# Parameter rows on GpSimd's queue, two more of the first weight strips on ScalarE's queue, and the first six GELUs ahead of the table sines

## The chip, the cores and the metric

The kernel runs on one core of one Trainium2 chip. The time is the device time of one execution in microseconds (us); lower is better. Before the change it is 216.26 us in the median of the 4 executions that were timed beside the changed kernel (216.15 to 216.58). The profiles show one execution each; the profiled span of the kernel before is 214.7 us, a little less than its time, because the span runs from the first to the last instruction.

Names used below: PE is TensorE, DVE is VectorE, ACT is ScalarE, POOL is GpSimd, SP is SyncE, which issues most of the DMAs. In the profile, PEld is PE's weight loads, and a q behind a name (SPq) is that engine's sequencer, which waits and issues. A "bank" is one of the eight PSUM banks of this kernel, into which PE writes. The "granted clock" is the share of full speed at which PE was allowed to run. In the code P is 128, a chunk has TPC = 4 tiles of 128 rows (H = 2, HT = 256), 640 columns are KD = KS = 5 blocks of 128, the 1728 are KF = 14 (the last one partial), and FA = 6 of these come first.

## The reference

The input x has 2048 rows of 640. The output mixes two branches with a gate computed from x:

```python
g = sigmoid((x * gate_w).sum(-1, keepdims=True))
# branch A: a diagonal complex state space model, 640 states
dt = exp(log_dt);  Lam_bar = exp(dt * Lam);  B_bar = ((Lam_bar - 1) / Lam)[:, None] * Bmat
h_t = Lam_bar * h_{t-1} + B_bar @ x_t            # a scan over the 2048 rows
a   = 2 * real(C @ h) + x * Dskip
# branch B: a dense layer, 640 -> 1728 -> 640
b   = gelu(x @ w1 + b1) @ w2 + b2
out = g * a + (1 - g) * b                        # bf16
```

## The kernel before

The rows are handled in four chunks of 512. The complex scan is made real by rotating with tables of cosines and sines (`TCOS`, `TSIN`), which the kernel itself builds at the start: ScalarE computes four small sine activations, and DVE multiplies them out. PE, DVE and ScalarE run in an order that is fixed by hand; SP's order is left to the framework.

The start: x's first chunk comes in four strips and is transposed on PE; `w1a` (the first 768 columns of w1) comes in five strips, `w1b` (the rest) in five more.

```python
load_xn(0, 0, 1)
load_w1a(nc.scalar, 0)
load_xn(0, 1, 2)
load_w1a(nc.scalar, 2)
...                                               # a tiny Exp, to load its table
load_xn(0, 2, 3)
load_xn(0, 3, 4)
rows(nc.sync, prmA[0:KS, :], A_log_dt)            # parameter rows, 1.2 to 3.2 KB each
rows(nc.sync, prmA[KS:2 * KS, :], A_Lambda_im)
rows(nc.sync, prmA[2 * KS:3 * KS, :], A_Lambda_re)
for kd in (1, 4, 3):
    load_w1a(nc.sync, kd)
rows(nc.sync, prmB[KS:NB, :], B_b1[0:(KF - 1) * P])
rows(nc.sync, prmB[0:KS, :], gate_w)
for kd in range(KD):                              # w1b
    nc.sync.dma_start(out=w1b[kd][:, 0:F - cut1], in_=B_w1[kd * P:(kd + 1) * P, cut1:F])
```

PE's order at the start is a mix of `strip` (matmuls of one w1a strip into six open banks) and `turn_all` (transposes of one x strip). The parameter rows are transposed by one matmul each (`prmA` gives `colA`, `prmB` gives `colB`, the GELU biases). Then come the four sines, then the six first GELUs:

```python
nc.scalar.activation(out=FS[...], in_=red,     func=ACT.Sin, ...)
nc.scalar.activation(out=FC[...], in_=ab,      func=ACT.Sin, ...)
nc.scalar.activation(out=sq[:],   in_=redq[:], func=ACT.Sin, ...)
nc.scalar.activation(out=cq[:],   in_=absq[:], func=ACT.Sin, ...)
for kf in range(FA):
    ...                                           # at kf == 3: prmB is transposed, colB copied
    for kd in (4, 3):
        ff1_mm(banks[kf], 0, kf, kd, 0, CH, False, 3)
for kf in range(FA):
    ff1_act(banks[kf], 0, kf)                     # GELU with bias colB: bank -> gel
...
nc.vector.tensor_tensor(out=m1, in0=FC[:, :, lo], in1=over(cQ), op=ALU.mult)   # DVE's first product with cq
```

`fold` rescales C in five steps; ScalarE makes two products in a pair of buffers (`ft`, `bufs=2`), DVE uses them:

```python
def fold(ks):
    t1 = fwork.tile([P, D], F32, name="ft", bufs=2)
    t2 = fwork.tile([P, D], F32, name="ft", bufs=2)
    nc.scalar.activation(out=t1[:], in_=CT_im[:, ks, :], func=ACT.Identity, scale=n2im[:, ks:ks + 1])
    nc.scalar.activation(out=t2[:], in_=CT_re[:, ks, :], func=ACT.Identity, scale=n2im[:, ks:ks + 1])
    ...                                           # DVE: CT_re <- CT_re * c2re + t1, CT_im <- CT_im * n2re + t2
```

`seed(ti)` lets DVE write x times Dskip into a bank, into which PE then accumulates the final tile `ti`; `fin_a` makes the output tile `ot` on DVE and stores it. `ot` has two buffers, and the loads of the next x chunk are issued right after:

```python
def fin_a(c, at={}):
    for a in range(TPC):
        ot = fwork.tile([P, D], BF16, name="ot", bufs=2)
        if a < TPC - 2:
            seed(ti + 2)
        ...                                       # matmuls; DVE: ot <- bank * gate + gb
        nc.sync.dma_start(out=out2d[ti * P:(ti + 1) * P, :], in_=ot[:])
...
fin_a(0)
load_xn(2, 0, H)
load_xn(2, H, TPC)
ssm(2, {KS - 1: lambda: first_banks(1)})
```

Of the kernel before, what the change touches and what calls it, by code (L numbers as in the profile page):

```python
# [11 lines left out]
ACT = mybir.ActivationFunctionType  # L12
# [4 lines left out]
P = 128  # L17
T = 2048
D = 640
F = 1728  # L20
CH = 512
NCH = T // CH
KD = D // P
KS = D // P
KF = (F + P - 1) // P
F_LAST = F - (KF - 1) * P
NT = T // P
TPC = CH // P
H = TPC // 2
HT = H * P  # L30
KSA = 2
HD = D // 2
FA = 6

MAGIC = 12582912.0
TWO_PI_M = float(np.float32(2.0 * np.pi * (1.0 - 2.0 ** -20)))
# [5 lines left out]
def kernel(  # L42
# [19 lines left out]
    nc = tc.nc  # L62
# [12 lines left out]
    def bank(dtype=F32):  # L75
        return ps.tile([P, CH * 4 // (4 if dtype == F32 else 2)], dtype, name="bank")


    cut1 = FA * P
    n1b = F - cut1 + 1  # L80
    xT = [const.tile([P, KD, CH], BF16, name=f"xT{c}") for c in range(NCH)]
    w1a = [const.tile([P, cut1], BF16, name=f"w1a_{kd}") for kd in range(KD)]
    w1b = [const.tile([P, n1b], BF16, name=f"w1b_{kd}") for kd in range(KD)]
# [6 lines left out]
    ident = const.tile([P, P], BF16, name="ident")  # L90
    prmA = const.tile([P, P], BF16, name="prmA")
    NB = KS + KF - 1
    prmB = const.tile([P, P], BF16, name="prmB")
    colA = const.tile([P, 3 * KS], F32, name="colA")
    colB = const.tile([P, NB], F32, name="colB")
# [10 lines left out]
    halfpi = const.tile([P, 1], F32, name="halfpi")  # L106
# [8 lines left out]
    def load_xn(c, a0=0, a1=TPC, queue=None):  # L115
        if a0 == 0:
            xn[c] = xnp.tile([P, TPC, D], BF16, name="xn")
        r0 = c * CH + a0 * P
        (queue or nc.sync).dma_start(out=xn[c][:, a0:a1, :], in_=x2d[r0:r0 + (a1 - a0) * P, :].rearrange("(a p) d -> p a d", p=P))

    def load_w1a(queue, kd):
        queue.dma_start(out=w1a[kd][:], in_=B_w1[kd * P:(kd + 1) * P, 0:cut1])

    def rows(queue, dst, v):
        queue.dma_start(out=dst, in_=v.rearrange("(j p) -> j p", p=P))  # L125
# [2 lines left out]
    load_w1a(nc.scalar, 0)  # L128
    load_xn(0, 1, 2)
    load_w1a(nc.scalar, 2)  # L130
    warm = const.tile([P, 1], F32, name="warm")
    nc.scalar.activation(out=warm[:], in_=nc.const_aps.tensor(1.0, [P, 1], BF16), func=ACT.Exp)
    load_xn(0, 2, 3)
    nc.vector.memset(prmA[:], 0.0)
    nc.vector.memset(prmB[:], 0.0)
    load_xn(0, 3, 4)
    rows(nc.sync, prmA[0:KS, :], A_log_dt)
    rows(nc.sync, prmA[KS:2 * KS, :], A_Lambda_im)
    rows(nc.sync, prmA[2 * KS:3 * KS, :], A_Lambda_re)
    for kd in (1, 4, 3):  # L140
        load_w1a(nc.sync, kd)
    rows(nc.sync, prmB[KS:NB, :], B_b1[0:(KF - 1) * P])
    rows(nc.sync, prmB[0:KS, :], gate_w)
    for kd in range(KD):
        nc.sync.dma_start(out=w1b[kd][:, 0:F - cut1], in_=B_w1[kd * P:(kd + 1) * P, cut1:F])  # L145
    make_identity(nc, ident[:])
    HC = CH // 4
    tfi = work.tile([P, HC], I32, name="e")
    nc.gpsimd.iota(tfi[:], pattern=[[1, HC]], base=0, channel_multiplier=0)
    nc.gpsimd.memset(b1x[:, F_LAST:F_LAST + 1], 0.0)  # L150
    span4 = const.tile([P, 4], F32, name="span4")
    for i, m in enumerate((1.0, float(CH), float(2 * HC), float(HC))):
# [5 lines left out]
    nc.sync.dma_start_transpose(out=xT[1][:], in_=x2d[CH:2 * CH, :])  # L158
    nc.sync.dma_start_transpose(out=CT_re[:], in_=A_C_re[:, :])
    nc.sync.dma_start_transpose(out=CT_im[:], in_=A_C_im[:, :])  # L160
    for k0, k1 in ((0, 3), (3, 6), (6, 9), (9, KF - 1)):
        nc.sync.dma_start(out=w2_sb[:, k0:k1, :], in_=B_w2[k0 * P:k1 * P, :].rearrange("(kf p) d -> p kf d", p=P))
    for h in range(2):
        nc.sync.dma_start(out=w2l[h * F_LAST:(h + 1) * F_LAST, :], in_=B_w2[(KF - 1) * P:F, :])
# [1 line left out]
    nc.sync.dma_start(out=Dbc[:], in_=A_Dskip.rearrange("(o d) -> o d", o=1).to_broadcast([P, D]))  # L166
    nc.sync.dma_start_transpose(out=xT[2][:], in_=x2d[2 * CH:3 * CH, :])
    nc.sync.dma_start_transpose(out=xT[3][:], in_=x2d[3 * CH:4 * CH, :])
    for a in (0, H):
        load_xn(1, a, a + H)  # L170

    ctx.enter_context(tc.manual_schedule(engines={E.PE, E.DVE, E.Activation}))

# [39 lines left out]
    pA = bank()  # L213
# [43 lines left out]
    def ff1_act(p, c, kf):  # L257
        nc.scalar.activation(out=gel[c][:, kf, :], in_=p[:, :], func=ACT.Gelu_apprx_tanh, bias=b1_c[:, kf:kf + 1])  # L258
        act(0.69)
# [51 lines left out]
    def strip(kd, t0, t1, first, f0=0, f1=FA):  # L311
        for kf in range(f0, f1):
            ff1_mm(banks[kf], 0, kf, kd, t0, t1, first, 3)

    def turn_all(a):
        tB = bank()
        for i in range(3):
            turn(tB, i * P, a, i)
        turned(nc.vector, tB, 0, a, 0, 1)
        turned(nc.vector, tB, P, a, 1, 3)  # L320
        for i in range(2):
            turn(pA, i * P, a, 3 + i)
        turned(nc.scalar, pA, 0, a, 3, 5)
# [2 lines left out]
    turn_all(1)  # L326
    strip(2, 0, P, False)
    strip(0, P, HT, True)
    nc.tensor.matmul(pA[:, HT:HT + 3 * KS], lhsT=prmA[:], rhs=ident[:, 0:3 * KS], start=True, stop=True, skip_group_check=True)
    nc.vector.tensor_copy(out=colA[:], in_=pA[:, HT:HT + 3 * KS])  # L330
    nc.scalar.activation(out=dt16[:], in_=ldt_c, func=ACT.Exp)
    strip(2, P, HT, False, 0, 3)
    turn_all(2)
    nc.vector.tensor_copy(out=dt32[:], in_=dt16[:])
    nc.vector.tensor_tensor(out=dtl[:], in0=dt32[:], in1=lre_c, op=ALU.mult)
    nc.vector.tensor_tensor(out=th_c[:], in0=dt32[:], in1=lim_c, op=ALU.mult)
    nc.vector.tensor_scalar(out=thp_c[:], in0=th_c[:], scalar1=INV_2PI, scalar2=None, op0=ALU.mult)
    strip(2, P, HT, False, 3, FA)
    strip(0, HT, HT + P, True)
    turn_all(3)  # L340
    nc.scalar.activation(out=r_c[:], in_=dtl[:], func=ACT.Exp)
    strip(2, HT, HT + P, False)
    strip(0, HT + P, CH, True)
    strip(2, HT + P, CH, False)
    strip(1, 0, CH, False)


    HB = 2 * HC
# [4 lines left out]
    u, red, ab = scratch(0), scratch(1), scratch(2)  # L353
    m1, m2 = scratch(3), scratch(4)
    FSC = hsp.tile([P, 2 * KS, HB], F32, name="hs")
    FS = FSC[:, 0:KS, :]
    FC = FSC[:, KS:2 * KS, :]
# [3 lines left out]
    redq = col("redq", n=NQ * KS)  # L361
    absq = col("absq", n=NQ * KS)
    sq = col("sq", n=NQ * KS)
    cq = col("cq", n=NQ * KS)
# [11 lines left out]
    sQ, cQ = sq[:, 3 * KS:4 * KS], cq[:, 3 * KS:4 * KS]  # L376


    nc.scalar.activation(out=FS[:, :, 0:HC], in_=red, func=ACT.Sin, scale=TWO_PI_M)
    nc.vector.scalar_tensor_tensor(out=ab, in0=red, scalar=-1.0, in1=red, op0=ALU.mult, op1=ALU.max)  # L380
    nc.scalar.activation(out=FC[:, :, 0:HC], in_=ab, func=ACT.Sin, scale=-TWO_PI_M, bias=halfpi[:])
    nc.vector.tensor_tensor(out=two[:].rearrange("p (n k) -> p n k", n=NQ), in0=thp_c[:].rearrange("p (o k) -> p o k", o=1).to_broadcast([P, NQ, KS]),
                            in1=span4[:].rearrange("p (n o) -> p n o", o=1).to_broadcast([P, NQ, KS]), op=ALU.mult)
    nc.vector.tensor_copy(out=kq[:], in_=two[:])
    nc.vector.tensor_tensor(out=redq[:], in0=two[:], in1=kq[:], op=ALU.subtract)
    nc.vector.scalar_tensor_tensor(out=absq[:], in0=redq[:], scalar=-1.0, in1=redq[:], op0=ALU.mult, op1=ALU.max)
    nc.scalar.activation(out=sq[:], in_=redq[:], func=ACT.Sin, scale=TWO_PI_M)
    nc.scalar.activation(out=cq[:], in_=absq[:], func=ACT.Sin, scale=-TWO_PI_M, bias=halfpi[:])
    for kf in range(FA):
        if kf == 3:  # L390
            nc.tensor.matmul(pA[:, 0:NB], lhsT=prmB[:], rhs=ident[:, 0:NB], start=True, stop=True, skip_group_check=True)
            nc.vector.tensor_copy(out=colB[:], in_=pA[:, 0:NB])
            for j in range(KD):
                nc.vector.tensor_copy(out=w1b[j][:, n1b - 1:n1b], in_=pA[:, j:j + 1])
        for kd in (4, 3):
            ff1_mm(banks[kf], 0, kf, kd, 0, CH, False, 3)
    for kf in range(FA):
        ff1_act(banks[kf], 0, kf)
    two_banks = [bank(), bank()]
    for kd in range(KD):  # L400
        for i in range(2):
# [278 lines left out]
    ff1(2, 0, {1: lambda: fold(3), 4: lambda: fold(4), 9: lambda: seed(0), 11: lambda: seed(1)})  # L680
    gates(2)
    fin_a(0)
    load_xn(2, 0, H)
    load_xn(2, H, TPC)
    ssm(2, {KS - 1: lambda: first_banks(1)})
    fin_b(1, seeds(1))
    fin_a(1)
    load_xn(3, 0, H)
    load_xn(3, H, TPC)
    ssm(3)  # L690
    gel_tile(3)
    ff1(3, 0, {KF - 3: lambda: first_banks(2)})
# [36 lines left out]
```

## Time and profile before

| | before |
|---|---|
| time, median of 4 | 216.26 us |
| span of the profiled execution | 214.7 us |
| PE busy | 209.7 us, 98% |
| DVE busy | 190.2 us, 89% |
| sines done (end of the one at 12.53 us), first GELU | 12.83 us, 14.14 us |
| DVE's first product with `cq` | 12.86 us |

The profile page of before gives the busy time of each engine, and the shares of the chain of waits that ended last:

```profile
span 214.7 us, 3536 instructions
...
PE 209.7 (98%) x1366; PEld 117.1 (55%) x1385; DVE 190.2 (89%) x396; ACT 101.4 (47%) x183; POOL 1.1 (0%) x12
...
PE 93%; DMA 3%; SPq 1%; issue 1%; DVE 0%
```

PE is the limit, but DVE is close behind it. DVE's order is fixed, so a delay at its start travels on until a moment at which it would have waited anyway.

The timeline of ScalarE in before; columns are start, duration (both us), engine, line, operation and tiles, and in brackets the idle time before it and what ended it:

```profile
8.66 1.28 ACT L379 ACT_TABLE_LOAD   x1
10.83 0.74 ACT L379 ACTIVATE hs<-gel 128x640 f32<-128x640 f32 x1 [0.88 <-DVE gel L372]
...
12.53 0.30 ACT L388 ACTIVATE cq<-absq,halfpi 128x20 f32<-128x20 f32 x1
12.84 1.28 ACT L258 ACT_TABLE_LOAD   x1
14.14 0.69 ACT L258 ACTIVATE gel<-bank,colB 128x512 bf16<-128x512 f32 x1
```

The sine table is loaded at 8.66 us, while the first sine still waits for DVE until 10.83.

The timeline of PE in before, the one place at the start where PE waits for a weight:

```profile
12.97 1.89 PE L253 MATMUL bank<-xT,w1b 128*128 128x512 bf16 x8
15.09 1.25 PE L253 MATMUL bank<-xT,w1b 128*128 128x512 bf16 x5 [0.23 <-DMA w1b<-in_B_w_dram]
```

The timeline of DVE in before: the product that needs `cq`, and the three longest waits of its steady part.

```profile
12.86 0.83 DVE L408 TENSOR_TENSOR gel<-hs,cq 128x640 f32<-128x640 f32 x1
...
76.19 0.89 DVE L459 SCALAR_TENSOR_TENSOR CT_re<-CT_re,c2re,ft 128x640 bf16<-128x640 bf16 x1 [0.38 <-ACT ft L455]
...
88.12 0.17 DVE L551 TENSOR_SCALAR gcol<-gz 128x4 f32<-128x4 f32 x1 [0.88 <-ACT gz L285]
...
97.34 0.55 DVE L658 SCALAR_TENSOR_TENSOR ot<-bank,gcol,gb 128x320 bf16<-128x320 f32 x1 [0.33 <-DMA out_dram<-ot]
```

The last one is a wait for a buffer of `ot`, whose store has not landed. The table of waits of before between 60 and 110 us (total, times, longest) has one more line for the argument: ScalarE waits 1.2 us for DVE to free an `ft` buffer, without any effect on PE.

```profile
ACT ft L453 <- DVE CT_re L459: 1.2, 1, 1.2
```

### The profile page before, as it was taken

To read this page: it belongs to the slowest core of one execution; us is meant where nothing else is said; L and a number is where in the kernel's file an instruction comes from. 1 tells how busy PE (TensorE), PEld (TensorE's weight loads), DVE (VectorE), ACT (ScalarE), POOL (GpSimd) and SP (SyncE) were. 2 spreads that over 40 slices of the span, in tenths; PEclk is the share of its full clock that TensorE was granted. 3 is DMA by queue.
4 is the path that set the end of the run, shared out by engine and by line. 5 is a ranking of instruction groups with operands and counts; after the bars stand their busy time and mean duration, and the time that the engine had idled before them with its cause. 6 is when DMAs were issued, how large, how long until landed. Compare 5 with 4: busy or idle time off the path is not lost.

```text
span 214.7 us, 3536 instructions
## 1 busy us (share of the span) xinstructions
PE 209.7 (98%) x1366; PEld 117.1 (55%) x1385; DVE 190.2 (89%) x396; ACT 101.4 (47%) x183; POOL 1.1 (0%) x12
## 2 busy tenths in 40 slices
PE   8999999999999999999999999999999999999994
PEld 4745444454455644775445577444454567654774
DVE  2899999999999999899999999999999999983153
ACT  3599556665875696302572310356683423204200
POOL 1000000000000000000000000000000000000000
PEclk9999999999999999999999999999999999999999
DMA  6899999993000000051000005100000000100011
GB/s 201 251 177 232 219 220 374 170 225 92 3 0 0 3 2 0 12 183 64 0 0 3 0 0 186 61 2 0 0 3 14 0 3 31 61 31 3 0 66 61
DMA packets 30419, 15.84 MB, mean 74 GB/s; under 512 B 22978, under 2 KB 30402, under 8 KB 30402
## 3 DMA queue, kind: packets, MB, share of 16 engines
q1 hardware_dynamic: 29970, 15.18, 29.3%
q10 hardware_dynamic: 432, 0.43, 0.6%
q8 instruction: 11, 0.18, 0.3%
q14 instruction: 6, 0.05, 0.1%
HBM read 7.48 MB, written 2.62 MB: 47 GB/s over the span
## 4 chain that ended last, share of the span: by engine, by line
PE 93%; DMA 3%; SPq 1%; issue 1%; DVE 0%
PE bank L594 26%; PE bank L253 23%; PE bank L653 20%; PE bank L536 20%; DMA w1b<-in_B_w_dram 3%; PE bank L215 1%; PE bank L610 1%; PE bank L279 1%; SPq L145 1%; PE bank L218 0%; SPq L125 0%; DVE ot L658 0%; DVE xT L225 0%; PE bank L269 0%
## 5 line engine op out<-in xcount | busy, mean ns | idle before, releaser
L594 PE MATMUL bank<-w_sb,gel 128*128 128x128 bf16 (+1 forms) x408 | 56.9, 297 | 0.7 <-issue 0.5
L594 PEld LDWEIGHTS <-gel 128*128 128x128 bf16 x416 | 32.2, 98 | 25.5
L539 ACT ACTIVATE bu<-bank 128x512 bf16<-128x512 f32 x40 | 23.9, 597 | 39.4 <-PE bank L536 39.3
L258 ACT ACTIVATE gel<-bank,colB 128x512 bf16<-128x512 f32 x52 | 34.1, 694 | 11.9 <-PE bank L253 11.1
L653 PEld LDWEIGHTS <-hs 128*128 128x128 bf16 x330 | 31.6, 98 | 11.5
L490 DVE TENSOR_TENSOR_SCAN g<-r_c,carry,v 128x512 bf16<-128x512 f32 x30 | 37.4, 1272 | 0.0
L602 ACT ACTIVATE gb<-bank,gcol 128x512 f32<-128x512 f32 (+1 forms) x32 | 15.1, 527 | 35.4 <-PE bank L610 19.3
L253 PE MATMUL bank<-xT,w1b 128*128 128x512 bf16 x137 | 31.0, 379 | 0.4 <-DMA w1b<-in_B_w_dram 0.2
L253 PE MATMUL bank<-xT,w1a 128*128 128x512 bf16 (+1 forms) x152 | 27.7, 334 | 0.2
L653 PE MATMUL bank<-CT_re,hs 128*128 128x320 bf16 (+2 forms) x165 | 27.1, 295 | 0.0
L653 PE MATMUL bank<-CT_im,hs 128*128 128x320 bf16 (+2 forms) x165 | 27.1, 295 | 0.0
L658 DVE SCALAR_TENSOR_TENSOR ot<-bank,gcol,gb 128x320 bf16<-128x320 f32 (+2 forms) x33 | 17.6, 535 | 9.2 <-PE bank L653 8.7
L536 PE MATMUL bank<-xT,BT_im 128*128 128x512 bf16 x99 | 24.8, 379 | 0.1
L536 PE MATMUL bank<-xT,BT_re 128*128 128x512 bf16 x97 | 24.4, 379 | 0.2
L253 PEld LDWEIGHTS <-w1b 128*128 128x128 bf16 x140 | 13.6, 98 | 16.9 <-DMA w1b<-in_B_w_dram 0.7
L253 PEld LDWEIGHTS <-w1a 128*128 128x128 bf16 x156 | 13.8, 101 | 12.5
L569 DVE TENSOR_TENSOR bank<-xn,Dbc 128x320 f32<-128x320 bf16 (+2 forms) x33 | 14.5, 483 | 3.5 <-ACT gb L602 3.4
L536 PEld LDWEIGHTS <-BT_im 128*128 128x128 bf16 x100 | 9.8, 98 | 11.8
L471 DVE TENSOR_TENSOR v<-wa,wb 128x512 bf16<-128x512 bf16 x40 | 15.2, 421 | 0.6
L536 PEld LDWEIGHTS <-BT_re 128*128 128x128 bf16 x100 | 9.6, 98 | 11.0
L583 ACT ACTIVATE bank<-b2bc 128x512 f32<-128x512 bf16 (+1 forms) x24 | 11.7, 529 | 6.2 <-DVE ot L658 6.2
L471 DVE TENSOR_TENSOR wa<-TCOS,g 128x1024 bf16<-128x1024 bf16 x20 | 13.7, 687 | 0.1
(100 smaller groups left out, 151.5 us busy)
## 6 DMA issues: line engine op xcount, KB each, us to landing
out_dram<-ot SPq DMA_DIRECT2D x15, 160.0 KB, 1.8
xn<-in_A_x_dram SPq DMA_DIRECT2D x6, 320.0 KB, 3.2
w_sb<-in_B_w_dram SPq DMA_DIRECT2D x3, 480.0 KB, 4.0
w1b<-in_B_w_dram SPq DMA_DIRECT2D x5, 240.0 KB, 6.1
xn<-in_A_x_dram SPq DMA_DIRECT2D x4, 160.0 KB, 3.1
w_sb<-in_B_w_dram SPq DMA_DIRECT2D x1, 640.0 KB
w1a<-in_B_w_dram SPq DMA_DIRECT2D x3, 192.0 KB, 2.9
w1a<-in_B_w_dram ACTq DMA_DIRECT2D x2, 192.0 KB, 3.6
```

What stands on the lines that cost most here:

```text
L253: nc.tensor.matmul(p[:, t0:t1], lhsT=w, rhs=xT[c][:, kd, t0:t1], start=(kd == 0) if first is None else first, stop=(kd == last), skip_grou ...
L258: nc.scalar.activation(out=gel[c][:, kf, :], in_=p[:, :], func=ACT.Gelu_apprx_tanh, bias=b1_c[:, kf:kf + 1])
L471: nc.vector.tensor_tensor(out=o, in0=a, in1=b, op=op)
L490: nc.vector.tensor_tensor_scan(s["g"][:, ri, :], r_c[:, ks:ks + 1].to_broadcast([P, CH]), s["v"][:, ri, :], init, ALU.mult, ALU.add)
L536: nc.tensor.matmul(p[:], lhsT=BT[ks >= KSA][:, kd, (ks % KSA if ks < KSA else ks - KSA) * P:][:, 0:P], rhs=xT[c][:, kd, :], start=(kd == 0 ...
L539: nc.scalar.activation(out=bu[:, ri, :], in_=p[:], func=ACT.Identity)
L569: dve_now(ck.pe, 0.45, lambda: nc.vector.tensor_tensor(out=p[:, 0:d1 - d0], in0=xn[c][:, a, d0:d1], in1=Dbc[:, d0:d1], op=ALU.mult))
L583: nc.scalar.activation(out=v, in_=src, func=ACT.Identity)
L594: nc.tensor.matmul(p[:, col:col + d1 - d0], lhsT=gel[c][:, kf, a * P:(a + 1) * P], rhs=w2_sb[:, kf, d0:d1], start=False, stop=False, skip_ ...
L602: nc.scalar.activation(out=gbs[ti][:, d0:d1], in_=p[:, col:col + d1 - d0], func=ACT.Identity, scale=gcol[:, 1, ti:ti + 1])
L653: nc.tensor.matmul(p[:, 0:d1 - d0], lhsT=hs[c][:, j, lo:lo + P], rhs=CT[:, j % KS, d0:d1], start=False, stop=(j == 2 * KS - 1), skip_group ...
L658: nc.vector.scalar_tensor_tensor(out=ot[:, d0:d1], in0=p[:, 0:d1 - d0], scalar=gcol[:, 0, ti:ti + 1], in1=gbs[ti][:, d0:d1], op0=ALU.mult, ...
```

## The change

The intent: take small DMAs off SP's queue so that the weights are issued earlier; close the first six banks and let ScalarE empty them before the sines, so that PE gets banks back sooner; and spread loads over more pieces.

```diff
 load_w1a(nc.scalar, 2)
+load_w1a(nc.scalar, 1)
+load_w1a(nc.scalar, 4)
 ...
-rows(nc.sync, prmA[0:KS, :], A_log_dt)                 # and the two others
-for kd in (1, 4, 3):
-    load_w1a(nc.sync, kd)
-rows(nc.sync, prmB[KS:NB, :], B_b1[0:(KF - 1) * P])    # and gate_w
+load_w1a(nc.sync, 3)
 ...                                                    # w1b on nc.sync, as before
+rows(nc.gpsimd, prmA[0:KS, :], A_log_dt)               # and the four others, on nc.gpsimd
 ...
-for k0, k1 in ((0, 3), (3, 6), (6, 9), (9, KF - 1)):                       # w2
+for k0, k1 in ((0, 2), (2, 4), (4, 6), (6, 8), (8, 10), (10, KF - 1)):
 ...
-for a in (0, H):
-    load_xn(1, a, a + H)
+load_xn_in_3(1)                                        # three pieces; also for chunks 2 and 3
 ...
 strip(0, P, HT, True)
+strip(2, P, HT, False, 0, 3)
+turn_all(2)
+strip(2, P, HT, False, 3, FA)
 nc.tensor.matmul(pA[...], lhsT=prmA[:], ...)           # moved back behind them
 ...                                                    # colA, dt
+strip(0, HT, HT + P, True)
+turn_all(3)
 ...
 strip(1, 0, CH, False)
+nc.tensor.matmul(pA[:, 0:NB], lhsT=prmB[:], ...)       # moved ahead of the sines' DVE work
+nc.vector.tensor_copy(out=colB[:], in_=pA[:, 0:NB])
 ...
-nc.scalar.activation(... ACT.Sin ...)                  # the four sines
 for kf in range(FA):
     for kd in (4, 3):
         ff1_mm(banks[kf], 0, kf, kd, 0, CH, False, 3)
 for kf in range(FA):
     ff1_act(banks[kf], 0, kf)
+nc.scalar.activation(... ACT.Sin ...)                  # the four sines
```

More of the change, by code (lines that the diff above doesn't have):

```diff
@@ L119, in load_xn, with load_xn_in_3 @@
         (queue or nc.sync).dma_start(out=xn[c][:, a0:a1, :], in_=x2d[r0:r0 + (a1 - a0) * P, :].rearrange("(a p) d -> p a d", p=P))
+    def load_xn_in_3(c):
+        for a0, a1 in ((0, H), (H, H + 1), (H + 1, TPC)):
+            load_xn(c, a0, a1)
     def load_w1a(queue, kd):
@@ L136, with load_w1b @@
     load_xn(0, 3, 4)
-    rows(nc.sync, prmA[0:KS, :], A_log_dt)
-    rows(nc.sync, prmA[KS:2 * KS, :], A_Lambda_im)
-    rows(nc.sync, prmA[2 * KS:3 * KS, :], A_Lambda_re)
-    for kd in (1, 4, 3):
-        load_w1a(nc.sync, kd)
-    rows(nc.sync, prmB[KS:NB, :], B_b1[0:(KF - 1) * P])
-    rows(nc.sync, prmB[0:KS, :], gate_w)
+    load_w1a(nc.sync, 3)
+    def load_w1b(kd):
+        nc.sync.dma_start(out=w1b[kd][:, 0:F - cut1], in_=B_w1[kd * P:(kd + 1) * P, cut1:F])
     for kd in range(KD):
-        nc.sync.dma_start(out=w1b[kd][:, 0:F - cut1], in_=B_w1[kd * P:(kd + 1) * P, cut1:F])
+        load_w1b(kd)
     make_identity(nc, ident[:])
@@ L149 @@
     nc.gpsimd.iota(tfi[:], pattern=[[1, HC]], base=0, channel_multiplier=0)
+    rows(nc.gpsimd, prmA[0:KS, :], A_log_dt)
+    rows(nc.gpsimd, prmA[KS:2 * KS, :], A_Lambda_im)
+    rows(nc.gpsimd, prmA[2 * KS:3 * KS, :], A_Lambda_re)
+    rows(nc.gpsimd, prmB[KS:NB, :], B_b1[0:(KF - 1) * P])
+    rows(nc.gpsimd, prmB[0:KS, :], gate_w)
     nc.gpsimd.memset(b1x[:, F_LAST:F_LAST + 1], 0.0)
@@ L331 @@
     nc.scalar.activation(out=dt16[:], in_=ldt_c, func=ACT.Exp)
-    strip(2, P, HT, False, 0, 3)
-    turn_all(2)
+    strip(0, HT, HT + P, True)
+    turn_all(3)
     nc.vector.tensor_copy(out=dt32[:], in_=dt16[:])
@@ L337 @@
     nc.vector.tensor_scalar(out=thp_c[:], in0=th_c[:], scalar1=INV_2PI, scalar2=None, op0=ALU.mult)
-    strip(2, P, HT, False, 3, FA)
-    strip(0, HT, HT + P, True)
-    turn_all(3)
     nc.scalar.activation(out=r_c[:], in_=dtl[:], func=ACT.Exp)
@@ L345 @@
     strip(1, 0, CH, False)
+    nc.tensor.matmul(pA[:, 0:NB], lhsT=prmB[:], rhs=ident[:, 0:NB], start=True, stop=True, skip_group_check=True)
+    nc.vector.tensor_copy(out=colB[:], in_=pA[:, 0:NB])
+    for j in range(KD):
+        nc.vector.tensor_copy(out=w1b[j][:, n1b - 1:n1b], in_=pA[:, j:j + 1])
     HB = 2 * HC
@@ L376 @@
     sQ, cQ = sq[:, 3 * KS:4 * KS], cq[:, 3 * KS:4 * KS]
-    nc.scalar.activation(out=FS[:, :, 0:HC], in_=red, func=ACT.Sin, scale=TWO_PI_M)
     nc.vector.scalar_tensor_tensor(out=ab, in0=red, scalar=-1.0, in1=red, op0=ALU.mult, op1=ALU.max)
-    nc.scalar.activation(out=FC[:, :, 0:HC], in_=ab, func=ACT.Sin, scale=-TWO_PI_M, bias=halfpi[:])
     nc.vector.tensor_tensor(out=two[:].rearrange("p (n k) -> p n k", n=NQ), in0=thp_c[:].rearrange("p (o k) -> p o k", o=1).to_broadcast([P, NQ, KS]),
@@ L386 @@
     nc.vector.scalar_tensor_tensor(out=absq[:], in0=redq[:], scalar=-1.0, in1=redq[:], op0=ALU.mult, op1=ALU.max)
-    nc.scalar.activation(out=sq[:], in_=redq[:], func=ACT.Sin, scale=TWO_PI_M)
-    nc.scalar.activation(out=cq[:], in_=absq[:], func=ACT.Sin, scale=-TWO_PI_M, bias=halfpi[:])
     for kf in range(FA):
-        if kf == 3:
-            nc.tensor.matmul(pA[:, 0:NB], lhsT=prmB[:], rhs=ident[:, 0:NB], start=True, stop=True, skip_group_check=True)
-            nc.vector.tensor_copy(out=colB[:], in_=pA[:, 0:NB])
-            for j in range(KD):
-                nc.vector.tensor_copy(out=w1b[j][:, n1b - 1:n1b], in_=pA[:, j:j + 1])
         for kd in (4, 3):
@@ L398 @@
         ff1_act(banks[kf], 0, kf)
+    nc.scalar.activation(out=FS[:, :, 0:HC], in_=red, func=ACT.Sin, scale=TWO_PI_M)
+    nc.scalar.activation(out=FC[:, :, 0:HC], in_=ab, func=ACT.Sin, scale=-TWO_PI_M, bias=halfpi[:])
+    nc.scalar.activation(out=sq[:], in_=redq[:], func=ACT.Sin, scale=TWO_PI_M)
+    nc.scalar.activation(out=cq[:], in_=absq[:], func=ACT.Sin, scale=-TWO_PI_M, bias=halfpi[:])
     two_banks = [bank(), bank()]
@@ L682 @@
     fin_a(0)
-    load_xn(2, 0, H)
-    load_xn(2, H, TPC)
+    load_xn_in_3(2)
     ssm(2, {KS - 1: lambda: first_banks(1)})
@@ L687 @@
     fin_a(1)
-    load_xn(3, 0, H)
-    load_xn(3, H, TPC)
+    load_xn_in_3(3)
     ssm(3)
```

## The prediction

> **What bounds the kernel now.** The chain of waits is 93% PE, and the page shows PE busy 98% of 214.7 us. The timeline of matmul starts shows a 512-column matmul every 0.216 us and very few holes: about 0.5 us of small waits for the transposed first strips (6.7 to 8.4 us) and 0.39 us of waiting for the last w1b piece (it lands at 15.05 us; matmul due 14.70, started 15.09). The first x tile (3.7 us) and the half matmul rate until 5.9 us stay. So at most about 1 us can be won on PE.
>
> The timeline of DVE shows a fixed order with almost no idle time from 7 to 192 us. Its only real waits there are 0.29, 0.38 (for ScalarE's fold products), 0.88 us (88.1, for the gate) and 0.33 us (97.3, a store).
>
> **What the change does.**
> 1. Queues: five parameter rows (0.26 to 0.37 us of SP issue each) leave SP, and two w1a pieces move to ScalarE's queue. w1b issue starts near 3 us, not 6.3. The DMA engines are about 90% busy from 2 us, so pieces land only somewhat earlier; I expect the 0.39 us wait to go. GpSimd's rows may land later than SP's; the prmA transpose moves back about 0.8 us to allow it. The Trainium skill ("DMA: Bandwidth & Descriptors", Latency) gives the GpSimd path a later first byte; no trace here shows it yet. More load pieces: nothing critical. Sum: 0.3 to 0.7 us gained by 15 us.
> 2. GELU before sine. Before: sine table load 8.66 (1.28 us), four sines done at 12.83, GELU table 12.84, first GELU 14.14. After: the GELU table loads near 9; GELUs start when bank 0 closes (about 11 us), six at 0.60 us: until about 14.6. Then sine table 1.28, sines 1.8, GELU table 1.28. There are as many table loads, but the sines end near 17.6, not 12.83. ScalarE catches up before PE lacks banks.
> 3. DVE builds the cos/sin tables from these sines (first instruction 12.86). It will idle to about 17.6: about 4.7 us late.
>
> **How much is critical.** That delay D travels down DVE's fixed order. Waits at 76.2 and 88.1 (and partly 97.3) absorb about 1.4 us, leaving some 3.3 us. PE meets DVE where final tiles are seeded (bank<-xn,Dbc). Slack there now, from seed end to PE's first use: tile 0 4.6 us, tile 4 3.2, tile 8 2.4, tile 9 1.7 us (seed half done at 176.33, wanted at 178.09). So PE should stall about 1.6 us near 175 to 179 us, in place of the 0.5 us won at the start; ScalarE's waits for DVE in the folds may stall PE briefly near 84.
>
> If that slack reading is wrong, about 215.7 us; if right (three in four), about 218.
>
> **Prediction: 217.5 us, 80% range 215.6 to 218.7.** Faster by over 2%: 0.01; within 2%: 0.96; slower by over 2%: 0.03.
>
> **What the profile would show.** Right: w1b's wait near 15 us gone; ScalarE's groups with GELUs at 11 to 15 us, sine table after; DVE idle about 5 us before its first product with cq; all later DVE work 3 to 5 us late; new PE waits on the seed line at tiles 8 and 9, none on w1b. Wrong: DVE's products start near 13 us, or no PE wait on DVE at 175 us.
>
> **What would make it wrong.** GpSimd's rows landing after 8 us would stall PE; transposes issued earlier might slow w1b; DVE might absorb more of the delay; bank reuse in the folds might stall PE more than the seeds.

## The result, and the profile after

| | before | after |
|---|---|---|
| time, median of 4 | 216.26 us (216.15 to 216.58) | 222.06 us (221.42 to 222.44) |
| ratio after/before | | 1.0263, 95% interval 1.0236 to 1.0289 |
| span of the profiled execution | 214.7 us | 219.6 us |
| PE busy | 209.7 us, 98% | 209.5 us, 95% |
| DVE's first product with `cq` | 12.86 us | 19.46 us |

A ratio here and below is the mean time of one kernel's runs over that of the other's of the same rounds, so it is not quite the ratio of the medians that are quoted. The change made the kernel 2.6% slower, and the time lies outside the predicted range. The profile of before is of an execution of 216.61 us, above all four that were timed, and that of after is of the fastest, 221.42 us; so what is read from these two profiles is about 1.0 us less than the 5.80 us between the medians.

The page of after:

```profile
span 219.6 us, 3548 instructions
...
PE 209.5 (95%) x1366; PEld 116.7 (53%) x1385; DVE 190.0 (87%) x396; ACT 101.4 (46%) x184; POOL 3.8 (2%) x17
...
DVE 70%; PE 17%; ACT 5%; DMA 4%; issue 3%; SPq 0%; DVEq 0%; ACTq 0%
```

The work is the same, 209.5 us on PE and 190.0 on DVE. What is new is that the chain that ended last is 70% DVE, not 93% PE: PE now waits for a late DVE.

The timeline of ScalarE in after:

```profile
11.47 1.28 ACT L265 ACT_TABLE_LOAD   x1 [1.66 <-DVE colB L354]
12.77 3.58 ACT L265 ACTIVATE gel<-bank,colB 128x512 bf16<-128x512 f32 x6
16.36 1.28 ACT L401 ACT_TABLE_LOAD   x1
...
19.13 0.30 ACT L404 ACTIVATE cq<-absq,halfpi 128x20 f32<-128x20 f32 x1
19.44 1.28 ACT L265 ACT_TABLE_LOAD   x1
```

ScalarE was idle for 1.66 us and only then began to load the GELU table. In before, the load of the sine table ran during the wait of its first user; here it comes after the wait for `colB`.

The timeline of DVE in after, the lines that answer to those of before:

```profile
15.24 0.18 DVE L395 SCALAR_TENSOR_TENSOR absq<-redq 128x20 f32<-128x20 f32 x1
19.46 0.83 DVE L414 TENSOR_TENSOR gel<-hs,cq 128x640 f32<-128x640 f32 x1 [4.04 <-ACT cq L404]
...
82.08 0.88 DVE L465 SCALAR_TENSOR_TENSOR CT_re<-CT_re,c2re,ft 128x640 bf16<-128x640 bf16 x1
...
93.04 0.16 DVE L557 TENSOR_SCALAR gcol<-gz 128x4 f32<-128x4 f32 x1
...
103.68 0.55 DVE L664 SCALAR_TENSOR_TENSOR ot<-bank,gcol,gb 128x320 bf16<-128x320 f32 x1 [1.76 <-DMA out_dram<-ot]
```

DVE's lateness, the start of the same DVE instruction in after minus its start in before, is 19.46 - 12.86 = 6.60 us at the tables. At the places where DVE used to wait it shrinks, and the waits at 76.19 and 88.12 us of before are gone: 6.38 us at 70.85 us of before's time, 5.89 at 76.19, 4.92 at 88.12. At the store wait (97.34 us in before, 103.68 in after) it grows again, to 6.34 us: the wait did not absorb its 0.33 us, it became 1.76.

The timeline of PE in after, at the places where it stands still:

```profile
7.02 0.45 PE L225 MATMUL bank<-ident,xn 128*128 128x128 bf16 x5 [1.11 <-DMA xn<-in_A_x_dram]
...
82.26 1.67 PE L260 MATMUL bank<-xT,w1b 128*128 128x512 bf16 x7
85.30 1.24 PE L260 MATMUL bank<-xT,w1b 128*128 128x512 bf16 x4 [1.37 <-ACT gel L265]
87.62 1.24 PE L260 MATMUL bank<-xT,w1b 128*128 128x512 bf16 x5 [1.07 <-ACT gel L265]
...
179.38 0.84 PE L659 MATMUL bank<-CT_re,hs 128*128 128x320 bf16 x5 [0.69 <-DVE bank L575]
...
182.76 0.84 PE L659 MATMUL bank<-CT_re,hs 128*128 128x320 bf16 x5 [0.50 <-DVE bank L575]
```

The wait for w1b at 15 us is gone (the last piece landed at 11.85 us, not 15.04). PE lost time at five places. The table follows PE's own lateness: the start of the same matmul in after minus its start in before.

| where (us of before's time) | PE late by | what was added there |
|---|---|---|
| 72.8 | +0.22 us | the head: a wait for the third x strip, against a won w1b wait |
| 87.4, first final tile | +2.99 us | 2.77 us, waiting for banks at 83 to 88 us |
| 123.9 | +3.33 us | 0.34 us, seed of tile 4 |
| 175.2 | +4.17 us | 0.84 us, seed of tile 8 |
| 186.1 and to the end | +4.83 us | 0.66 us, seed of tile 9 |

The table of waits of after between 60 and 110 us says why the banks were missing:

```profile
ACT ft L459 <- DVE CT_re L465: 10.6, 3, 7.6
...
PE bank L260 <- ACT gel L265: 2.4, 2, 1.4
...
DVE ot L664 <- DMA out_dram<-ot: 1.8, 1, 1.8
```

ScalarE stands in `fold` for 10.6 us (1.2 us before) until the late DVE frees one of the two `ft` buffers. The GELUs that would empty PE's banks stand behind it in ScalarE's fixed order, and PE runs out of banks. The profile counts 2.44 us of this (1.37 + 1.07) from the modelled end of the last matmul; each of the two holes also costs some 0.16 us more, since back-to-back matmuls start 0.216 us apart and their records last 0.38. That makes the 2.77 us.

The theory after this reading had four parts: (a) GELU-first makes DVE late by 6.6 us; (b) part is absorbed, but the store wait gives some back; (c) the fold turns DVE's lateness into missing banks; (d) the seeds turn the rest into PE stalls. The rivals were that the load half (GpSimd's rows, two w1a strips on ScalarE's queue, more pieces) makes the loss; that the third load piece makes the store wait; and that a delay of DVE as such costs little, the loss being something particular to the new order.

### The profile page after: what moved, and what is told of

It is laid out like the page before. It is cut to its first block, busy times and chain, and to the rows that moved or that the text cites. A ratio compares the mean times of both kernels' runs of the same rounds, so it can differ in the third digit from the quotient of the medians.

```text
span 219.6 us, 3548 instructions
## 1 busy us (share of the span) xinstructions
PE 209.5 (95%) x1366; PEld 116.7 (53%) x1385; DVE 190.0 (87%) x396; ACT 101.4 (46%) x184; POOL 3.8 (2%) x17
## 4 chain that ended last, share of the span: by engine, by line
DVE 70%; PE 17%; ACT 5%; DMA 4%; issue 3%; SPq 0%; DVEq 0%; ACTq 0%
DVE g L496 18%; DVE wa L477 10%; DVE wb L477 10%; PE bank L659 9%; PE bank L600 6%; DVE v L477 6%; DVE hs L477 5%; DVE ot L664 3%; DVE bank L575 3%; DMA xn<-in_A_x_dram 2%; DVE CT_re L465 2%; ACT gel L265 2%; DVE CT_im L465 1%; DVE g L427 1%; PE bank L260 1%
## 5 line engine op out<-in xcount | busy, mean ns | idle before, releaser
L265 ACT ACTIVATE gel<-bank,colB 128x512 bf16<-128x512 f32 x52 | 33.6, 691 | 9.7 <-PE bank L260 9.6
L664 DVE SCALAR_TENSOR_TENSOR ot<-bank,gcol,gb 128x320 bf16<-128x320 f32 (+2 forms) x33 | 17.5, 532 | 10.6 <-PE bank L659 8.7
```

The lines of the kernel that those rows point to most:

```text
L265: nc.scalar.activation(out=gel[c][:, kf, :], in_=p[:, :], func=ACT.Gelu_apprx_tanh, bias=b1_c[:, kf:kf + 1])
L664: nc.vector.scalar_tensor_tensor(out=ot[:, d0:d1], in0=p[:, 0:d1 - d0], scalar=gcol[:, 0, ti:ti + 1], in1=gbs[ti][:, d0:d1], op0=ALU.mult, ...
```

## The experiments

All fifteen runs gave right results. Lateness is read as above, against the profile of before. Where nothing else is said, 4 executions of the experiment were timed.

### Each half alone

`a_loads` has the load half of the change (everything up to PE's fixed order, and the three-piece loads) on the compute order of before. `a_compute` is the reverse.

```diff
 # a_loads: before, with
+load_w1a(nc.scalar, 1); load_w1a(nc.scalar, 4); rows(nc.gpsimd, ...); load_xn_in_3(c); w2 in 6 pieces
 # a_compute: before, with
+prmA and prmB matmuls moved; six GELUs, then the four sines
```

> Only the load half of the change (queues, rows by GpSimd, more pieces) on the compute order of before. Theory (sines and thus VectorE late is the main cause): the third x strip lands near 7 us and stalls PE about 1.3 us, the late prmA rows start VectorE's table work about 1.3 us late, w1b's 0.39 us wait goes; VectorE's lateness stays under its slack, so 217.0 us (216.3 to 218.0). Rival (loads are the main cause): 220 us or more.

> Only the compute half (GELUs before sines, prmA and prmB transposes moved) on the loads of before. Theory: VectorE's first product with cq starts about 6 us later than 12.86, waits absorb about 1.3 us, slack at tile 9 is 1.7 us: 219.2 us (218.3 to 220.2). Rival (loads): under 217 us.

`a_loads`: 218.59 us, ratio 1.0101 (1.0070 to 1.0131). It is worse than expected (216.3 to 218.0): before's order asks for `prmA` early, GpSimd's rows are late, and a long store wait that had not been counted comes on top. The timeline of PE in `a_loads`:

```profile
5.09 0.93 PE L260 MATMUL bank<-xT,w1a 128*128 128x128 bf16 x12
7.63 0.17 PE L336 MATMUL bank<-ident,prmA 128*128 128x15 bf16 x1 [1.61 <-DMA prmA<-in_A_Lambda_re_dram]
```

So the change was right to move the `prmA` matmul back when it moved these rows. In this profiled execution PE also ran at half its clock for about 3 us afterwards (granted clock 0.50 from 8 to 10 us); the other executions had a mean clock of 1.00 and took 217.82 to 218.69 us. DVE was 1.97 us late, its store wait was 2.48 us here too, and PE ended 2.74 us late. None of DVE's lateness was absorbed at 76 and 88 us (it stayed at 2.05 us); PE itself was 2.05 us late there.

`a_compute`: 221.03 us, ratio 1.0214 (1.0182 to 1.0246), above the expected range, which had not counted a longer store wait. DVE was 6.18 us late at the tables, 4.50 us before the store, and 6.47 us after a store wait of 2.33 us. PE was 0.20 us early at 72.8 us, 2.56 us late at 87.4 and 5.04 us late at the end. The compute half alone thus shows the whole pattern of after: it is the main cause. The load half alone costs 1.0%, and the two do not add up (2.1% and 1.0% against 2.6%). The store wait also grows here with two load pieces, so a third piece is not needed for it.

### The third piece

`after_two_pieces` is after with x loaded in two pieces per chunk again.

```diff
-load_xn_in_3(c)
+load_xn(c, 0, H); load_xn(c, H, TPC)
```

> After with the x loads of chunks 1 to 3 in two pieces again. Theory: the third piece's issue took 2.33 us and held back a store, for which VectorE waited 1.76 us at 103.7; with two pieces that wait shrinks to about 0.3 us and the time falls by about 1.4 us, to 220.6 us (220.1 to 221.2). Rival (the store wait only reuses time that VectorE would lose anyway): within 0.3 us of after, 222.0.

A miss: 223.13 us, ratio 1.0298 (1.0269 to 1.0328). The store wait stayed, at 1.88 us, and a second one of 0.82 us appeared at 141.67 us. The third piece is not the cause.

### The late table load

`after_early_table` puts a one-element GELU behind the last Exp, so that the table is loaded while ScalarE has nothing to do.

```diff
 nc.scalar.activation(out=r_c[:], in_=dtl[:], func=ACT.Exp)
+nc.scalar.activation(out=warm2[:], in_=nc.const_aps.tensor(1.0, [P, 1], BF16), func=ACT.Gelu_apprx_tanh)
```

> After with a one-column GELU on a constant, right behind the last Exp, so that the GELU table loads near 9.9 us rather than behind the wait for colB at 11.47. Theory: first GELU near 11.6 rather than 12.77, everything behind it 1.1 us earlier, time 221.0 us (220.6 to 221.5). Rival (the table load is not what held the GELUs; bank 0 was): no change, 222.0.

220.50 us, ratio 1.0187 (1.0156 to 1.0219). The timeline of ScalarE in this run, against the load at 11.47 and the GELU at 12.77 us of after:

```profile
9.68 1.28 ACT L350 ACT_TABLE_LOAD   x1
...
11.50 3.58 ACT L265 ACTIVATE gel<-bank,colB 128x512 bf16<-128x512 f32 x6 [0.32 <-PE bank L260]
```

DVE's lateness fell to 5.33 us, that is by 1.27, the length of one table load. Its store wait was again large (2.25 us), and PE ended 4.23 us late.

### The sines first again

`after_sines_first` keeps everything of after but puts the four sines back ahead of the six GELUs.

```diff
-six GELUs; four sines
+four sines; six GELUs
```

> After with the four sines back in front of the six GELUs on ScalarE, nothing else undone. VectorE's own order still has colB (11.2 us) in front of the table angles, so the sines should end near 15.9 us and VectorE's first product start about 3.0 us later than in before. Theory (time follows that lateness, less about 1.3 us absorbed, plus about 1.4 us for the store wait, less 1.7 us slack): 218 us (217.2 to 219.0). Rival (order of sines and GELUs does not matter): 222.

219.66 us, ratio 1.0173 (1.0142 to 1.0204). A miss: DVE was only 2.36 us late, but a new stall stands in PE's timeline of this run. So 4.24 of after's 6.60 us come from the order of sines and GELUs. The other 2.36 come from what else stands ahead: DVE waits 1.36 us for the earlier `prmB` matmul and makes `colB` before it starts on the angles, at 10.95 us instead of 8.59 in before.

```profile
12.91 2.32 PE L260 MATMUL bank<-xT,w1b 128*128 128x512 bf16 x10
17.23 5.08 PE L260 MATMUL bank<-xT,w1b 128*128 128x512 bf16 x15 [2.01 <-ACT gel L265]
```

PE waits 2.01 us for an emptied bank, and from 18.5 to 21.9 us 512-column matmuls start 0.427 us apart instead of 0.216, so that PE was 3.39 us late by 21.6 us. (The other three executions kept a mean clock of 1.000 and took 219.29 to 219.82 us.) The intent of the change was therefore real: emptying the banks first does help PE at 15 us. It buys this with DVE's start. In before the sines were ready early enough for both.

### The first w1a strips

`after_w1a_sp` puts w1a strips 1 and 4 back on SP.

```diff
-load_w1a(nc.scalar, 1); load_w1a(nc.scalar, 4); load_w1a(nc.sync, 3)
+for kd in (1, 4, 3): load_w1a(nc.sync, kd)
```

> After with the w1a pieces 1 and 4 back on SP's queue behind the x strips. Theory: strip 2 of x lands near 4.9 us rather than 6.98, the 1.28 us PE stall at 7.02 goes; GELUs and sines start 0.3 to 0.5 us earlier only, since colB (GpSimd rows) gates them: 221.4 us (220.8 to 222.0). If strips were what delays the sines most: 220.7 or less.

221.24 us, ratio 1.0236 (1.0213 to 1.0260), an interval that overlaps after's. The 1.11 us wait for the x strip is gone; a wait of 0.30 us ahead of the `prmA` matmul, as in after, is left. In after that x strip, issued at 1.65 us, landed at 6.98, after 5.33 us, with the two w1a strips and GpSimd's rows in flight; in before it took 3.55 us (the sixteenth increment of its semaphore came at 5.20). With w1a back on SP it still took 4.71 us. The timeline of PE in this run:

```profile
5.50 1.59 PE L259 MATMUL bank<-xT,w1a 128*128 128x128 bf16 x15
6.92 0.44 PE L224 MATMUL bank<-ident,xn 128*128 128x128 bf16 x5
```

The transposes of the strip start at 6.92 us, only 0.10 us earlier than in after: in this execution 128-column matmuls were 0.107 us apart until about 6.7 us (0.054 in after from 4.2 us on), and these slower matmuls fill much of the time of the wait. The Trainium skill ("DMA: Bandwidth & Descriptors", Issuing engines are not separate DMA queues) says that the queues share the same 16 engines. So w1a on ScalarE's queue saved SP's issue time and probably took bandwidth from the strip that PE wanted first; how much is not shown, since this strip took 3.98 us in `after_sines_first`, with w1a on ScalarE's queue, and 3.74 in `after_all`, with it on SP. The end of the kernel hardly noticed: DVE was 6.48 us late all the same, and PE 0.11 us at 72.8 us and 4.94 at the end.

### A dose of delay in the kernel before

`dose4` and `dose8` are before with DVE's first product with `cq` computed 4 or 8 more times. This delays DVE by a known amount at just the place where after delays it, and changes nothing else.

```diff
 nc.vector.tensor_tensor(out=m1, in0=FC[:, :, lo], in1=over(cQ), op=ALU.mult)
+for _ in range(4):        # 8 in dose8
+    nc.vector.tensor_tensor(out=m1, in0=FC[:, :, lo], in1=over(cQ), op=ALU.mult)
```

> Before with the first product with cq repeated four more times on VectorE (same result): about 3.1 us of delay at 13 us, ScalarE untouched. Theory: about 1.3 us absorbed, 1.7 us slack at tile 9: PE shifted by 0 to 0.4 us, 216.5 us (216.2 to 217.0). Rival (every microsecond of VectorE delay reaches the end): 219.4.

> The same with eight more: about 6.2 us of delay. Theory: 6.2 - 1.3 - 1.7 = 3.2 us, 219.5 us (218.8 to 220.2), with PE waits on the seeds near 180 us and on ScalarE's GELUs near 85 us. Rivals: no effect (216.3), or all of it (222.5).

`dose8` delayed DVE by 6.59 us and took 221.60 us, ratio 1.0252 (1.0232 to 1.0272), as after does with 6.60 us of lateness and 1.0263. The delay as such makes the loss, and the rival of something particular to the new order falls. It is above the expected 218.8 to 220.2 us, since the store wait grew here too, to 2.10 us. The timeline of PE in `dose8`:

```profile
85.31 1.81 PE L253 MATMUL bank<-xT,w1b 128*128 128x512 bf16 x4 [2.28 <-ACT gel L258]
87.62 3.11 PE L253 MATMUL bank<-xT,w1b 128*128 128x512 bf16 x10 [0.51 <-ACT gel L258]
```

The granted clock fell to 0.50 behind the first stall, and all four executions of `dose8` had a mean clock of 0.991 or 0.992, against two of four in after. So the two times agree more closely than the two courses do. In this profile the fall does not set the end: PE was 3.79 us late at 88 us, and DVE's seeds near 180 us then made it 5.39 (DVE's 6.68 after the store, less 1.29).

`dose4` delayed DVE by 3.16 us and took 218.43 us, ratio 1.0099 (1.0074 to 1.0125), where 216.5 had been expected. Its lateness went 3.16, 2.97, 2.48 and, at 88 us, 1.51, all as expected; then the store wait was 2.55 us and the lateness 3.72. A little lateness of DVE made the wait longer than the lateness itself.

### Why the store wait grows

SP issues the stores of the four tiles and the loads of the next x chunk in the framework's order. In before the store of tile 1 was issued at 93.73 us, 0.55 us behind the two x loads, and DVE's wait for it ended at 97.34. In `dose4` it was issued at 95.23, again behind the two loads (94.26 and 94.68), and the wait ended at 101.06. The store shares the DMA engines with two loads of 320 KB each. `dose4_late` fixes SP's order by hand and lets the loads come behind the stores:

```diff
-ctx.enter_context(tc.manual_schedule(engines={E.PE, E.DVE, E.Activation}))
+ctx.enter_context(tc.manual_schedule(engines={E.PE, E.DVE, E.Activation, E.SP}))
 ...
 fin_a(0)
-load_xn(2, 0, H); load_xn(2, H, TPC)
 ssm(2, {KS - 1: lambda: first_banks(1)})
+load_xn(2, 0, H); load_xn(2, H, TPC)             # chunk 3 likewise
```

> The 3.1 us of VectorE delay again, but with the x loads of chunks 2 and 3 issued after the four stores of chunks 0 and 1 instead of between them (SP's order fixed by hand). Theory (the lateness is amplified at 97 us because a store behind the x loads lands 4 to 6 us after its issue, and VectorE needs its buffer): the store lands about 1.8 us after issue, VectorE's wait of 2.55 us there is gone, its lag stays near 1.2 us, below the slack of 1.6 us: 216.2 us (215.9 to 216.8). Rival (the slack at the seeds was simply over-read): 218.4 as in dose4.

216.17 us, ratio 1.0006 (0.9993 to 1.0019): the whole loss of `dose4` is gone. The same instructions in DVE's timeline, first of `dose4`, then of `dose4_late`:

```profile
97.83 0.68 DVE L473 TENSOR_TENSOR wb<-TSIN,g 128x1024 bf16<-128x1024 bf16 x1
101.06 0.55 DVE L660 SCALAR_TENSOR_TENSOR ot<-bank,gcol,gb 128x320 bf16<-128x320 f32 x1 [2.55 <-DMA out_dram<-ot]
```

```profile
97.76 0.68 DVE L473 TENSOR_TENSOR wb<-TSIN,g 128x1024 bf16<-128x1024 bf16 x1
98.36 0.54 DVE L660 SCALAR_TENSOR_TENSOR ot<-bank,gcol,gb 128x320 bf16<-128x320 f32 x1
```

The stores now land 1.8 to 2.3 us after issue, DVE is 1.01 us late afterwards, and PE never meets it. This also measures DVE's slack: a lateness of 1.0 us costs nothing.

Why the loads hurt so much more in `dose4` than in before is not fully settled. The store's semaphore shows that one share of it was late: in `dose8`, 15 of its 16 increments had come by 102.24 us and the last came at 103.93 (in `dose4` 99.06 and 100.97; in before 97.21 and 97.25). The Trainium skill says the same of the counting ("DMA: Bandwidth & Descriptors", Why a DMA increments its semaphore by 16 and not by 1: the engines finish independently, and only the full 16 means that all data landed). What held up that one share may be the fetch of PE's instructions, a 16 KB packet on a queue of its own that takes 0.9 to 2.1 us (once 2.9), about every 20 us. It came at 96.53 us in before, just as the store ended, and in the middle of the loads and the store in the others: 96.91 in `dose4`, 101.58 in `dose8`, 98.71 in after. `before_warm26` tests this by shifting the fetches: it warms PE up with more but shorter matmuls, 26 of 128 columns. These are 18 more, each with its weight load, so that PE's later instructions shift by 36.

```diff
-for n in (512, 512, 512, 512, 512, 512, 128, 128):
+for n in (128,) * 26:
```

> Before with the warm-up matmuls (six of 512 columns and two of 128) cut into 26 of 128: same warm-up time, 36 more PE instructions, so the 16 KB instruction fetch seen at 96.5 us should come about 2.4 us earlier, into the x loads, with VectorE not delayed at all. Theory (that fetch occupies one of the 16 DMA engines and holds back its share of the load and store): the wait of the first output of tile 3, 0.33 us in before, grows to 1 to 2.3 us; the time stays within 216.0 to 216.9 us since the slack hides most of it. Rival (the wait grows only with VectorE's lag): the wait stays near 0.3 us.

The fetch moved to 91.84 us, by 4.7 us and not by the expected 2.4, and the wait grew from 0.33 to 1.00 us; the time stayed at 215.97 us, ratio 1.0001 (0.9987 to 1.0016). But this run does not settle it. The wait ended at 97.45 us, nearly where it ends in before (97.34); it is longer because DVE came to it 0.56 us earlier while the store was issued no earlier (93.78 us), since the load ahead of it took SP 0.98 us to issue instead of 0.37. The fetch fell into the store of tile 0, which took 2.67 us to land instead of 1.83, so it may have caused that; the packets' records do not say which DMA engine carried them. The fetch as a cause stays an inference. The long wait has two visible forms: a store that lands late (5.05 us after issue in `after_two_pieces`), and an SP that is slow to issue what is ahead of it (the third x piece took 2.33 us to issue in after, so that the store left at 101.04 us). Both come with the x loads ahead of the store, and `dose4_late` shows that without these there is no wait.

### The same repair in after

> After with the same: x loads of chunks 2 and 3 behind the stores. Theory: VectorE's lag stays near 4.6 us after 104 us instead of 6.34, less 1.55 slack: 219.2 us (218.7 to 219.9). Rival: 222.

`after_late` is after with SP's order of `dose4_late`: 220.31 us, ratio 1.0194 (1.0167 to 1.0221). The store wait is gone, DVE's lateness is 4.39 us afterwards and PE has no stall after 87.6 us: part (b) is removed, and about a quarter of the loss with it. Part (d) is not removed but hidden, since PE is by then as late as DVE; `after_late_ft4` below meets the seeds again. More is left than had been expected, all of it at 83 to 90 us. In this execution PE was 4.44 us late there, not 2.99, since the granted clock fell. The windows of PE in `after_late`; columns are the window, its length and PE's busy time (number of matmul records), the granted clock, the DMA share and GB/s:

```profile
83.00:85.00 2.00, 0.83 (x4) 1.00 0.00 0
85.00:87.00 2.00, 1.24 (x5) 1.00 0.00 0
87.00:89.00 2.00, 1.50 (x4) 0.57 0.00 0
89.00:91.00 2.00, 2.00 (x6) 0.57 0.02 4
```

Of the four executions of `after_late`, two had a mean clock of 0.992 (221.04 and 220.86 us) and two of 1.000 (219.27 and 219.75 us). The same holds for after: two of its four executions had 0.992 (222.44 and 222.07 us). A mean of 0.992 over 220 us is 1.76 us of lost clock, so about 3.5 us at half rate, worked out from the result. The profiled execution of after kept its clock.

`after_late_ft4` also gives the fold four buffers. They are bf16, so that they take the same room as two of f32; the output was still right.

```diff
-t1 = fwork.tile([P, D], F32, name="ft", bufs=2)
-t2 = fwork.tile([P, D], F32, name="ft", bufs=2)
+t1 = fwork.tile([P, D], BF16, name="ft", bufs=4)
+t2 = fwork.tile([P, D], BF16, name="ft", bufs=4)
```

> After with the x loads behind the stores and four fold buffers in bfloat16 instead of two in float32, so that ScalarE's fold products no longer wait for VectorE. Theory: the PE stalls at 83 to 88 us and the drop of the granted clock there go; PE then meets VectorE at the seed of tile 0 (lag 5.8 against slack 4.6: about 1.2 us) and at tile 9 (4.4 against 1.55: 2.85 us in all): 218.9 us (218.3 to 219.4), against 220.3 without the buffers. Rival (the stall at 83 us has another cause): 220.3.

219.12 us, ratio 1.0139 (1.0117 to 1.0161). The stall at 83 to 88 us is gone; the windows of PE in this run:

```profile
83.00:85.00 2.00, 2.00 (x11) 1.00 0.00 0
85.00:87.00 2.00, 2.00 (x11) 1.00 0.00 0
87.00:89.00 2.00, 1.34 (x25) 1.00 0.00 0
```

Part (c) is confirmed: ScalarE's wait in the fold is what made PE stall there. PE was only 0.42 us late at 72.8 us; DVE's lateness, 6.78 us at the tables and 4.72 at 88 us, now meets PE at the seed of tile 0 (0.82 us at 88.63), and PE ends 2.68 us late. The stall is smaller, not nil: DVE is as late as ever.

`after_all` adds the two repairs of the start, the early table and w1a strips 1 and 4 on SP.

> The same with the early GELU table load and w1a pieces 1 and 4 back on SP. Theory: VectorE starts about 5.2 us late instead of 6.6, about 1.65 us are absorbed, 1.55 us slack at tile 9, and about 0.4 us are left of the late first strips: 217.6 us (217.0 to 218.4). Rival (the terms do not add): 218.9 as without them.

217.04 us, ratio 1.0038 (1.0019 to 1.0057). DVE's lateness is 5.05 us at the tables, 2.99 at 88 us and 2.57 later; PE is 0.19 us early until 175 us and 0.94 us late at the end.

The controls are the same repairs in before, without the change:

```diff
 # before_late_ft4: before, with the loads behind the stores and four bf16 fold buffers
 # best1: before, with the loads behind the stores and
-rows(nc.sync, prmB[KS:NB, :], B_b1[0:(KF - 1) * P]); rows(nc.sync, prmB[0:KS, :], gate_w)
+rows(nc.gpsimd, prmB[KS:NB, :], B_b1[0:(KF - 1) * P]); rows(nc.gpsimd, prmB[0:KS, :], gate_w)
```

> Control: before with the x loads behind the stores and the four fold buffers. Theory: nothing on the critical path changes: 216.0 us (215.7 to 216.3). Rival (these edits bring a gain of their own): 215.5 or less.

> Before with the two prmB rows on GpSimd's queue (w1b issued about 0.75 us earlier) and the x loads of chunks 2 and 3 behind the stores. Theory: w1b's wait of 0.39 us goes in those executions that have it and no lateness arises elsewhere: 215.9 us (215.6 to 216.2). Rival: nothing gained, 216.2.

`before_late_ft4` took 216.20 us (6 executions), ratio 0.9994 (0.9977 to 1.0012): in before these repairs mend nothing, because PE does not meet these waits. `best1` took 216.50 us (6 executions), ratio 1.0024 (1.0012 to 1.0037), slightly slower: a miss, whose cause was not looked for. No version beat before beyond its interval.

### The ladder

| kernel | ratio to before | DVE late at the tables, after the store | PE late at the end |
|---|---|---|---|
| after | 1.0263 (1.0236 to 1.0289) | 6.60, 6.34 us | 4.83 us |
| after_late | 1.0194 (1.0167 to 1.0221) | 6.49, 4.39 us | 4.44 us, from 87 us on |
| after_late_ft4 | 1.0139 (1.0117 to 1.0161) | 6.78, 4.30 us | 2.68 us |
| after_all | 1.0038 (1.0019 to 1.0057) | 5.05, 2.57 us | 0.94 us |

Each repair of a named cause takes away a part of the loss, and no interval overlaps the next. In the profiles with a late DVE, PE's lateness at the end is DVE's lateness after the store less 1.3 to 1.6 us (after: 6.34 - 4.83 = 1.51; after_all: 2.57 - 0.94 = 1.63; dose4: 3.72 - 2.23 = 1.49), unless PE had already lost more at 83 to 90 us, as in after_late, or DVE waits for a second store, as in after_two_pieces.

## Why the prediction was right or wrong

It was wrong in size, by 4.6 us, and gave 0.03 to a slowdown of over 2%; much of the chain of causes that it named was right, and one link, the store wait, was not. In the words of the prediction:

- **"The chain of waits is 93% PE", and DVE with "a fixed order with almost no idle time".** Right, and the decisive reading: dose8 shows that a late DVE alone makes a loss of this size.
- **"I expect the 0.39 us wait to go."** Right; the last w1b piece landed at 11.85 us instead of 15.04.
- **"Sum: 0.3 to 0.7 us gained by 15 us."** Wrong. PE was 0.22 us late by 72.8 us. PE waited 1.11 us for the third x strip, which took 5.33 us to land instead of 3.55. The term that was left out is what the moved DMAs take from others in flight; which of them took it is not separated (4.71 us in after_w1a_sp). Its weight in the end time is small.
- **"After: the GELU table loads near 9; GELUs start when bank 0 closes (about 11 us)."** Wrong. The load started at 11.47 us, behind the wait of its user for `colB`; with the table loaded early the first GELU came at 11.50. So "D about 4.7 us" measured 6.60: 1.27 us is the table load (after_early_table), about 0.5 us the first GELU itself, later than assumed (11.50 us).
- **"Waits at 76.2 and 88.1 (and partly 97.3) absorb about 1.4 us."** Half right. Up to 88.1 us, 1.68 us was absorbed (6.60 to 4.92). The wait at 97.3 was read as slack and was the opposite: it is the end of a store, behind loads that SP issues first. It went from 0.33 to 1.76 us and gave back 1.42 (4.92 to 6.34). This wait for a DMA is no fixed date: it moves with the issue and with what else is in flight. dose4_late shows that.
- **"PE meets DVE where final tiles are seeded ... tile 9 1.7 us."** Right. The measured slack is 6.34 - 4.83 = 1.51 us, and stalls stand at tiles 8 and 9, 179.38 and 182.76 us. PE's lateness at the end, 4.83 us, is this slack subtracted from a lateness that was 6.34 us instead of the 3.3 that was predicted.
- **"ScalarE's waits for DVE in the folds may stall PE briefly near 84."** The mechanism was right, but it was 2.77 us and not brief, and entered the sum with zero. It does not simply add to the end: with the seeds alone PE would still end about 6.34 - 1.51 us late (an estimate; it was not run by itself). It does set the time where the store wait is repaired (after_late), and in the profiles of after_late and dose8 the clock fell right behind it.
- **The clock** was not considered. In some executions the granted clock halves for some us behind the stall at 83 to 88 us.

The step that failed is thus the middle of the sum: lateness in, 4.7 (measured 6.60); absorbed, 1.4 net (measured 0.26 net of the store: 6.60 - 6.34). The last step, slack 1.5 to 1.7, held. In numbers: 1.9 us more lateness, 1.1 us less absorbed, 0.2 us less slack and the 0.5 us of the head that was not won take the predicted 1.1 us to the 4.83 us of the profile; about 1.0 us more lies between these two profiles and the medians.

What stays open: whether the instruction fetch is what holds up the last share of the store; why the clock falls in some executions and not in others after the same stall; and how much of the head's 0.22 us is chance, since executions with before's head stood 0.45 to 0.7 us earlier in other profiles than in that of before. One source of this is visible. In the profile of before, 128-column matmuls were 0.107 us apart until 5.9 us; in those of dose4, dose8 and dose4_late they were 0.054 us apart from 4.4 us or earlier, and PE stood 0.67 to 0.71 us earlier. In after they were so from 4.2 us, so that, like for like, its head may have lost about 0.9 us (an estimate: 0.22 + 0.67).

## What to carry to other kernels

When an engine with a fixed order is nearly full, follow a delay through every place where it waits, and ask of each wait whether it is a date that stays (it absorbs) or something that starts later when the engine is late, such as a store that frees a buffer (it does not absorb, and may grow). Before an activation function of another table moves to a new place, see what its first user waits for, and load the table ahead with a one-element instruction if that wait is long. A queue of another engine saves issue time; the transfer still runs on the same DMA engines, as cited above, so ask what else is in flight when the first strips are wanted. Put bulk loads behind small stores that somebody waits for, as dose4_late did.

## What the Trainium skill lacked or had wrong

- "ScalarE: Activation LUTs", What ACT_TABLE_LOAD costs: the load of about 1283 ns agrees (1.28 us in every timeline here). The page adds about 1380 ns of drain, 2.66 us for every switch; here a switch cost 1.31 us from the last sine's end to the first GELU's start (12.83 to 14.14 us in before), so no such drain shows.
- The same page does not say on which side of its user's wait the load runs: in before the sine's load ran at 8.66 us, ahead of a wait that ended at 10.83; in after the GELU's load ran at 11.47 us, after a wait of 1.66 us of its user. Loading it early took 1.27 us off DVE's lateness (`after_early_table`).
- "TensorE: Matmul & The Clock Gate", Part 1: half rate and full rate agree (0.427 and 0.216 us between 512-column matmuls), and the about 3.5 us at half rate fit its window. But its advice, in Why this matters for your kernels, of no idle gaps over about 3 us is too loose: in `after_late` the clock fell after two stalls of 1.36 and 1.07 us by the profile, and in `dose8` after one of 2.28; in the profiled execution of after, stalls of 1.37 and 1.07 us left it at full rate.
- "DMA: Bandwidth & Descriptors", Latency and other measured facts, gives GpSimd's path a first byte after about 1 us. In after rows of 1.2 to 3.2 KB landed 4.7 to 5.1 us after issue with the engines busy (two x strips of 160 KB, issued by SP meanwhile, took 5.3 and 5.7); that is a landing and not a first byte, and no run here measured an idle queue.
- "Runtime: NRT & Kernel Launch", Instruction fetch mechanics, calls the refills mostly hidden. Here 16 KB packets of instructions took 0.9 to 2.1 us (once 2.9) of a DMA engine about every 20 us; that they delay one share of another transfer is an inference (in `dose8` 15 of 16 increments came by 102.24 us, the last at 103.93).
